# Attention scores from the queries as loaded: two 64x64 products per pair of heads in place of one 128x128 product, and a reordered second half of attention

## The chip, the cores and the metric

The kernel runs on one core of a Trainium2 chip as one program. The metric is the device time of that core in microseconds, the median over several runs, compared between kernels on the same chip. Engines are called as the profile calls them: PE (matrix products, with its weight loads PEld), DVE, ACT, POOL, and SP, which here only issues DMAs.

## What is computed

Three layers in a row, all in float32. First a local attention with block summaries, for 2 batches, 8 heads, 768 positions and head width 64:

```python
k_sum = k.reshape(B, H, nb, 32, D).max(axis=3)
v_sum = v.reshape(B, H, nb, 32, D).mean(axis=3)
scores_l = where(abs(i - j) < 16, scale * q @ k.T, -1e9)
scores_s = scale * q @ k_sum.T + log(32)
a = softmax(concat([scores_l, scores_s]))
x = a @ concat([v, v_sum])
```

Its rows become 1536 tokens of width 512. Then a mixture of 8 experts with one expert per token, `relu(x @ w1[e]) @ w2[e]` times two gates (widths 512, 1024, 512). Then a gated layer on all tokens, `(sigmoid(x @ w_gate) * (x @ w_val)) @ w_out` (widths 512, 1536, 512).

## The kernel before

**The program.** There is no scheduler: every engine executes its instructions in the order in which the Python code issues them, and waits on semaphores where data or buffers are not ready. Attention is the first sixth of the time. It overlaps with the load and the first steps of the experts. After it come seven blocks of up to 256 tokens each through an expert (`item_A` is the first product, `item_B` the second), and then the gated layer.

**Attention** goes over 12 tiles T of 128 queries (6 per batch), for all 8 heads. A tile has two halves of 64 queries, and each half meets its own 128 columns of keys (96 near keys or padding, and 24 block maxima) which stand in `kg` with two heads over each other: head 2p on partitions 0 to 63, head 2p+1 on 64 to 127. The steps of a tile are small functions:

- `load_q` (lines 226 to 228) brings 128 partitions x 512 queries: two heads over each other, 4 pairs, 2 halves, 64 queries. The buffers lie in `xg`, which later holds the tokens of the experts.
- `spread_q` (230 to 239) copies them, scaled by -0.125, into one of three `qz` buffers, as blocks of 128x128 with zeros in the two off-diagonal quarters. For T = 2 and 3 DVE does it, otherwise ACT, two instructions a tile. POOL zeroes the buffers once (line 833).
- `s1` (302 to 335): per half, a bfloat16 product writes the mask for all 4 pairs into a PSUM bank (line 312, full array), then 4 products of 128x128 by 128 columns add the scores, one for each pair (line 316). DVE takes the minimum (`nm`, line 333) and ACT the exponentials (335). Scores are negative here, so minimum and scale -1 stand for the maximum.
- `s3` (337 to 345): PE transposes the exponentials (`a`, line 344) and ACT copies them to `aT`. Two PSUM banks with the tag B serve these transposes and those of `s6`.
- `s4` (347 to 364): 16 products with 64 columns of weights and 65 moving columns (line 354), which write the upper and the lower 64 partitions of the bank pair C in turn; DVE normalises into `x`.
- `s6` and `s7` (366 to 380): transposes of `x` and the 16 router logits (379).

`place_sums` (281 to 294) turns the block means of v: 8 products with 24 columns of weights and 128 moving columns (line 286), to partitions 32 and 96 in turn.

A float32 product on PE stands as two records in the trace (two passes); transposes and the products of the experts, which use a reduced float32 type, stand as one.

**The loop over T** (856 to 974) runs `s1` two tiles ahead of `s4`. From T = 6 on it also carries the routing of the first batch (`route`, one step per `run(g, 1)`), from T = 7 the choice of the first two expert blocks (`pick_two`, a chain of small DVE instructions) and `find_first`, which finds the token rows of block 0: six comparisons of 128x256 on DVE (602), 12 small products on PE (607), and two gathers on POOL. At T = 10 and 11 the weights of block 0 are split into a high and a low part: `split1(p)` (628) is one ACT copy and one DVE subtraction for a quarter of `w1`. `item_T` transposes the tokens of block 0 for `item_A`.

Of the kernel before, what the change touches and what calls it, by code (L numbers as in the profile page):

```python
# [30 lines left out]
NT = B * TB  # L31
KST = 160
KW = TB * KST + 32
C = 128
# [34 lines left out]
def shape_constants():  # L69
    bf = lambda x: float(np.float32(x).astype(ml_dtypes.bfloat16))  # L70
    c = 8.0 * math.log(BLK)
    parts = []
    for _ in range(3):
        parts.append(bf(c))
        c -= parts[-1]
    mask = np.zeros((67, 4, C), np.float32)
    for v, t in ((0, 0), (1, 2), (2, 1), (3, 2 * TB - 1)):
        for c in range(C):
            col = col_start(t) + c
            k = key_of(col)  # L80
            if is_sum(col):
                mask[64:67, v, c] = [-0.125 * x for x in parts]
            elif k is None:
                mask[:64, v, c] = 1.0e9
            else:
                q = t * 64 + np.arange(64)
                mask[:64, v, c] = np.where(np.abs(q - k) < WIN, 0.0, 1.0e9)
    sel = np.zeros((67, 128), np.float32)
    sel[np.arange(128) % 64, np.arange(128)] = 1.0
    sel[64:] = 1.0  # L90
    m = np.zeros((80, 4 * C + 128), ml_dtypes.bfloat16)
    m[:67] = np.concatenate([mask.reshape(67, -1), sel], axis=1)
    kb = np.ones((128, CKB), ml_dtypes.bfloat16)
    kb[:, 0:128] = np.triu(np.ones((128, 128)), 1)
    kb[:, 256:256 + SLOT] = np.arange(SLOT)
    token = np.stack(np.broadcast_arrays(np.arange(128)[:, None], 128 * np.arange(TB)), axis=2)
    kb[:, 256 + SLOT:256 + SLOT + 2 * TB] = token.reshape(128, 2 * TB)
    k = np.zeros((128, 128), np.float32)
    e = np.arange(E)
    k[:, 0:8] = E - e  # L100
    k[:, 16:24] = e
    k[:, 24:88] = np.broadcast_to(np.arange(8)[None, :] * float(SLOT), (E, 8)).reshape(-1)
    k[:, 88:101] = np.arange(13)
    k[:, 101:114] = SLOT * np.arange(13)
    k[:, 114:127] = NTOK + SLOT * np.arange(13)
    return m, k, kb, np.eye(128, dtype=np.float32)


def moe_kernel(tc, A, out):
# [107 lines left out]
    qz = {}  # L217
    st = {}

    qbuf = [at.tile([128, 4, 2, 128], F32, name=f"qz{k}") for k in range(3)]  # L220
# [8 lines left out]

    def spread_q(T):  # L230

        qz[T] = qbuf[T % 3]
        src = q_raw(T).rearrange("p (g h q) -> p g h q", g=4, h=2)
        for j in range(2):
            s = slice(64 * j, 64 * j + 64)
            if 1 < T < 4:
                ts(qz[T][s, :, :, s], src[s], -0.125, ALU.mult)
            else:
                SC.mul(qz[T][s, :, :, s], src[s], -0.125)
# [62 lines left out]
    def s1(T, halves=(0, 1)):  # L302
# [11 lines left out]
        def score(half, pr):  # L314
            c0 = col_start(2 * m + half)
            PE.matmul(sc[half][:, pr], qz[T][:, pr, half], kg[b][:, pr, c0:c0 + C], start=False, stop=pr == 3)
# [9 lines left out]
        for half in halves:  # L326
            if T:
                mask(half)
                for pr in range(4):
                    score(half, pr)  # L330
            scv = sc[half]
            nm = at.tile([128, 4], F32, tag="nm", bufs=4, name=f"nm{T}{half}")
            pace.append(red(nm, scv, ALU.min))
            for pr in range(4):
                SC.activation(out=a[:, half * 4 + pr], in_=scv[:, pr], func=AF.Exp, bias=nm[:, pr:pr + 1], scale=-1.0)
# [260 lines left out]
    def find_first():  # L596
# [6 lines left out]
        yield  # L603
# [220 lines left out]
    with tc.manual_schedule():  # L824
# [7 lines left out]
        for t in qbuf:  # L832
            G.memset(t, 0.0)
# [16 lines left out]
        spread_q(0)  # L850
        spread_q(1)
# [3 lines left out]
        spread_q(2)  # L855
        for T in range(NT):
# [3 lines left out]
            if T < 2:  # L860
# [7 lines left out]
                if T == 1:  # L868
                    spread_q(3)
            else:  # L870
                if T < NT - 1:
                    s3(T)
                if T == 3:
                    spread_q(5)
# [3 lines left out]
                if T == NT - 1:  # L878
                    item_T(0, 0, ("A", 3))
                    item_T(0, 1, ("A", 3))  # L880
                    s4(T)
                    now = ()
                for t in q8:
                    s7(t)
                for t in now[:-1]:
                    s4(t)
                for t in first:
                    s1(t, (0,))
                for t in q6:
                    s6(t)  # L890
                if 2 < T < NT - 3:
                    spread_q(T + 3)
                for t in first:
                    s1(t, (1,))
                if T == 2:
                    spread_q(4)
                if T == 3:
                    ksum(1, 1)
                if T == 8:
                    run(ff, 9)  # L900
                if T > 8:
                    run(g, 1)
            for t in now[-1:]:
                s4(t)
            for t in then:
                s1(t)
# [8 lines left out]
            if T == 1:  # L915
# [3 lines left out]
                load_q(7)  # L919
# [12 lines left out]
            if T == 2:  # L932
                ksum(1, 0)
# [3 lines left out]
            if 2 < T < 7:  # L937
                load_q(T + 5)
            if T == 4:
                place_sums(1)  # L940
# [16 lines left out]
            if T == 7:  # L957
# [4 lines left out]
                run(ff, 1)  # L962
# [5 lines left out]
            if T == 10:  # L968
                split1(1)
                split1(2)  # L970
            if T == 11:
                run(g, 9)
                load_w(reg["e", 0], None, range(4, 8))
                split1(3)
# [10 lines left out]
        item_A(0)  # L985
        s6(11)
        item_A(1)
        run(p1, 1)
        item_gather(0, gidx[:, 16], S)
        item_gather(1, gidx[:, 17], S)  # L990
        item_A(2)
        s7(11)
        item_A(3)
# [263 lines left out]
```

## Time and profile before

| | |
|---|---|
| time of 3 runs | 551.37, 552.43, 552.91 us; median 552.43 |
| the profiled execution | 552.51 us, of which the trace spans 550.7 |
| PE busy | 535.1 us, 97% of the span |
| DVE, ACT, POOL busy | 386.8, 213.0, 124.7 us |
| granted PE clock, mean over the span | 0.994 of full speed |

The profile names a group of equal instructions by line, engine, operation and tiles. A busy PE is modelled: records last longer than the step from one to the next, so the pace of PE is read from the starts of neighbouring groups, not from the length of a record. In a timeline the bracket behind a row is the idle time of that engine before it and what ended it.

### The profile page before, as it was taken

The page shows a single profiled execution, that of the slowest core. Times are in us where ns is not written, and L with a number is a line of the kernel's source. Part 1 is how long each engine was busy: PE and PEld are TensorE (multiplying, and loading weights), DVE is VectorE, ACT ScalarE, POOL GpSimd, SP SyncE. Part 2 cuts the span into 40 slices and gives each one's busy share as a digit, 9 for nine tenths or more (in the row PEclk, how much of TensorE's full clock was granted, in tenths as well). Part 3 has the DMA queues.
Part 4 walks back from the last instruction along what each step waited for, and adds up shares of the span by engine and source line. Part 5 has one row for each costly group of instructions (what it writes and reads, how often), then busy time and mean ns, then how long its engine had stood idle before and what let it go on. Part 6 is the DMA issues. An engine that isn't in the chain of part 4 may idle for free.

```text
span 550.7 us, 8927 instructions
## 1 busy us (share of the span) xinstructions
PE 535.1 (97%) x3236; PEld 456.3 (83%) x3236; DVE 386.8 (70%) x737; ACT 213.0 (39%) x390; POOL 124.7 (23%) x151
## 2 busy tenths in 40 slices
PE   7999999999999999999999999999999999999995
PEld 4789989888989989878888888888888888888884
DVE  5785876898778677853878899999998753323330
ACT  3776683655546455643221221211111442122110
POOL 3656054072101101000010111102101152212211
PEclk9999998999999999999999999999999999999998
DMA  8994286971569403216132323323322000001001
GB/s 323 412 411 144 84 279 218 333 281 39 176 252 297 136 12 118 72 56 211 39 114 78 114 80 111 115 81 112 114 76 77 1 2 38 20 38 39 21 37 39
DMA packets 31984, 71.63 MB, mean 130 GB/s; under 512 B 3056, under 2 KB 11712, under 8 KB 31936
## 3 DMA queue, kind: packets, MB, share of 16 engines
q1 hardware_dynamic: 28816, 60.96, 32.1%
q0 software_dynamic: 3120, 10.06, 5.4%
q8 instruction: 26, 0.43, 0.3%
q14 instruction: 22, 0.18, 0.1%
HBM read 72.53 MB, written 11.33 MB: 152 GB/s over the span
## 4 chain that ended last, share of the span: by engine, by line
PE 34%; issue 15%; POOL 5%; ACT 0%; POOLq 0%; DVE 0%; DVEq 0%; ACTq 0%
PE ps_A L1141 18%; PE ps_B L1141 15%; POOL out_dram L1189 3%; POOL yb L134 2%; PE ps_B L746 1%; POOLq L1253 0%; ACT yb L131 0%; ACT gs L131 0%; DVE gg L137 0%; POOLq L1189 0%; DVEq L137 0%; POOLq L134 0%; ACTq L131 0%
## 5 line engine op out<-in xcount | busy, mean ns | idle before, releaser
L1182 PE MATMUL ps_A<-yb,gs 128*128 128x512 f32 x432 | 98.1, 389 | 0.0
L1141 PE MATMUL ps_A<-yb,wh 128*128 128x512 f32 x312 | 96.9, 392 | 0.1
L1182 PEld LDWEIGHTS ps_A<-yb,gs 128*128 128x128 f32 x432 | 81.1, 188 | 16.8
L1141 PE MATMUL ps_B<-yb,wh 128*128 128x512 f32 x264 | 81.3, 389 | 0.0
L1141 PEld LDWEIGHTS ps_A<-yb,wh 128*128 128x128 f32 x312 | 57.9, 188 | 12.0 <-issue 0.6
L1141 PE MATMUL ps_A<-yb,wl 128*128 128x512 f32 x156 | 60.8, 389 | 0.0
L1141 PEld LDWEIGHTS ps_B<-yb,wh 128*128 128x128 f32 x264 | 49.5, 188 | 10.2
L134 POOL TENSOR_TENSOR wl<-cvw,wh 128x512 fp32r<-128x512 f32 x20 | 26.7, 1334 | 137.8 <-ACT wh L131 137.8
L1150 ACT ACTIVATE sg<-ps_A 128x512 f32<-128x512 f32 x36 | 21.5, 596 | 91.2 <-PE ps_A L1141 91.2
L652 PE MATMUL ps_A<-xTh,w1h 128*128 128x256 f32 x192 | 55.4, 289 | 1.0 <-DVE hl L655 1.0
L652 PE MATMUL ps_A<-xTl,w1h 128*128 128x256 f32 x192 | 54.8, 286 | 0.0
L652 PE MATMUL ps_A<-xTh,w1l 128*128 128x256 f32 x192 | 54.8, 286 | 0.0
L1141 PE MATMUL ps_B<-yb,wl 128*128 128x512 f32 x132 | 51.3, 389 | 0.0
L131 ACT ACTIVATE gs<-gg 128x768 fp32r<-128x768 f32 x24 | 20.3, 847 | 69.5 <-PE ps_A L1182 67.4
L134 DVE TENSOR_TENSOR gs<-gg,gs 128x768 fp32r<-128x768 f32 x24 | 23.0, 958 | 34.2 <-ACT gs L131 34.1
L143 DVE TENSOR_SCALAR cva<-cva 128x512 f32<-128x512 f32 x72 | 43.4, 602 | 1.9
L134 DVE TENSOR_TENSOR w2l<-w2r,w2h 128x1024 fp32r<-128x1024 f32 x28 | 34.2, 1224 | 9.9 <-ACT w2h L131 9.6
L661 PE MATMUL yp<-w2h,hh 128*128 128x512 f32 x96 | 39.0, 406 | 0.0
L652 PEld LDWEIGHTS ps_A<-xTh,w1h 128*128 128x128 f32 x192 | 37.3, 194 | 1.6 <-DVE hl L655 1.4
L661 PE MATMUL yp<-w2h,hl 128*128 128x512 f32 x96 | 37.6, 391 | 0.0
L652 PEld LDWEIGHTS ps_A<-xTl,w1h 128*128 128x128 f32 x192 | 37.4, 195 | 0.2
L661 PE MATMUL yp<-w2l,hh 128*128 128x512 f32 x96 | 37.5, 391 | 0.0
(232 smaller groups left out, 959.3 us busy)
## 6 DMA issues: line engine op xcount, KB each, us to landing
w1r<-in_w_dram SPq DMA_DIRECT2D x28, 512.0 KB
w2r<-in_w_dram SPq DMA_DIRECT2D x28, 512.0 KB
raw<-in_wgv_dram SPq DMA_DIRECT2D x24, 512.0 KB
vt<-in_vv_dram SPq DMA_DIRECT2D x12, 520.0 KB
raw<-in_wo_dram SPq DMA_DIRECT2D x12, 512.0 KB
kg<-in_kg_dram SPq DMA_DIRECT2D x8, 496.0 KB
y_c<-yt SPq DMA_DIRECT2D x13, 256.5 KB
yr<-y_c SPq DMA_DIRECT2D x12, 256.5 KB
```

Source lines behind the costliest of these rows:

```text
L131: SC.activation(out=o, in_=i, func=AF.Copy)
L134: (eng or V).tensor_tensor(out=o, in0=i, in1=h.bitcast(F32), op=ALU.subtract)
L143: V.tensor_scalar(out=o, in0=a, scalar1=s1, scalar2=s2, op0=op0, op1=op1)
L652: PE.matmul(hp, w[:, c, s], x[:, c], start=n == 0, stop=n == 11)
L661: PE.matmul(yp[h], x[:, f, s], w[:, f], start=f == 0 and n == 0, stop=f == 7 and n == 2)
L746: PE.transpose(tp[:, c], r[:, c * 128:c * 128 + 128], ident)
L1141: PE.matmul(pp, w[:, c], x[:, c], start=n == 0, stop=n == 11)
L1150: SC.activation(out=sg, in_=pp, func=AF.Sigmoid)
L1182: PE.matmul(po, g2[:, x, f % 6], yb[f // 4][w][:, f % 4], start=f == 0 and n == 0, stop=f == 11 and n == 2)
L1189: d = G.indirect_dma_start(out=out[:, :], out_offset=bass.IndirectOffsetOnAxis(ap=row_id[:, t:t + 1].bitcast(U32), axis=0), in_=ot, in_off ...
```

## The change

`spread_q`, its three buffers and their zeroing go. Per pair of heads the score is now two products, one for each head, on 64 partitions of the queries as loaded and of the keys: rows 0 to 63 write PSUM partitions 0 to 63, and rows 64 to 127 write partitions 64 to 127 of the same bank. The queries are no longer scaled or negated, so the mask's constants change, the minimum becomes a maximum, DVE multiplies it by -0.125 in an instruction of its own, and the scale of the exponential is 0.125.

Query buffers now stay in use until the scores have been taken, so `load_q(7)` and `load_q(8)` to `load_q(11)` are issued one tile later. The order in the second half of attention changes too: `place_sums(1)` from the end of T = 4 to between the two halves of `s1` at T = 5; the comparisons of `find_first` in two groups of three, each behind a half of `s1` at T = 8, and its products behind `s4(8)`; at T = 10 `s7` between the transposes of tiles 10 and 11; at T = 11 `s4(11)` behind `s7(9)` and `s6(10)`; and the splits 1 to 3 of `w1` into the first items of block 0.

```diff
-                mask[64:67, v, c] = [-0.125 * x for x in parts]
+                mask[64:67, v, c] = parts
-    qbuf = [at.tile([128, 4, 2, 128], F32, name=f"qz{k}") for k in range(3)]
-    def spread_q(T):
...
-            PE.matmul(sc[half][:, pr], qz[T][:, pr, half], kg[b][:, pr, c0:c0 + C], start=False, stop=pr == 3)
+            q = q_raw(T).rearrange("p (g h q) -> p g h q", g=4, h=2)
+            for p0 in (0, 64):
+                r = slice(p0, p0 + 64)
+                PE.matmul(sc[half][r, pr], q[r, pr, half], kg[b][r, pr, c0:c0 + C], start=False, stop=pr == 3)
...
-            pace.append(red(nm, scv, ALU.min))
+            pace.append(red(nm, scv, ALU.max))
+            ts(nm, nm, -0.125, ALU.mult)
...
         for t in range(TB):
             ts(P[:, t], count, first, ALU.add, pf[:, t:t + 1], ALU.is_equal)
-        yield
+            if t % 3 == 2:
+                yield
...
+                if T == NT - 1:
+                    item_T(0, 0, ("A", 3))
+                    item_T(0, 1, ("A", 3))
+                for t in q8:
+                    s7(t)
                 if T == NT - 2:
                     s3(T + 1)
                     split1(0)
-                if T == NT - 1:
-                    item_T(0, 0, ("A", 3))
-                    item_T(0, 1, ("A", 3))
-                    s4(T)
-                    now = ()
-                for t in q8:
-                    s7(t)
                 for t in now[:-1]:
                     s4(t)
                 for t in first:
                     s1(t, (0,))
+                if T == 8:
+                    run(ff, 1)
                 for t in q6:
                     s6(t)
+                if T == 5:
+                    place_sums(1)
                 for t in first:
                     s1(t, (1,))
                 if T == 8:
-                    run(ff, 9)
+                    run(ff, 1)
                 if T > 8:
                     run(g, 1)
             for t in now[-1:]:
                 s4(t)
+            if T == 8:
+                run(ff, 9)
...
-            if 2 < T < 7:
-                load_q(T + 5)
+            if 3 < T < 8:
+                load_q(T + 4)
             if T == 4:
-                place_sums(1)
...
-            if T == 10:
-                split1(1)
-                split1(2)
             if T == 11:
                 run(g, 9)
                 load_w(reg["e", 0], None, range(4, 8))
-                split1(3)
...
         item_A(0)
+        split1(1)
         s6(11)
         item_A(1)
         run(p1, 1)
+        split1(2)
...
         s7(11)
+        split1(3)
         item_A(3)
```

PE at the end of attention, T = 10 and 11, in the order before (`a` exponentials, `xp` the output of `s4`, `late` the tokens, `xT` their transposes, `xg` the tokens of block 0):

```order
L354 MATMUL xp_1202<-vt_111,aT_1148 64x65 x16
L344 MATMUL ps_B<-ident,a_1059 128x128 x8
L344 MATMUL ps_B<-ident,a_1167 128x128 x8
L379 MATMUL ps_A<-wgo,xT_1185 128x16 x4
L370 MATMUL ps_B<-ident,late 128x128 x4
L354 MATMUL xp_1271<-vt_111,aT_1227 64x65 x16
L641 MATMUL ps_A<-ident,xg_87 128x128 x8
L354 MATMUL xp_1313<-vt_111,aT_1240 64x65 x16
L379 MATMUL ps_A<-wgo,xT_1266 128x16 x4
L370 MATMUL ps_B<-ident,late 128x128 x4
```

And the same place in the changed kernel, whose line numbers are smaller by about ten:

```order
L305 MATMUL ps_A<-kg_107,xg_88 64x128 x8
L344 MATMUL xp_1292<-vt_111,aT_1228 64x65 x16
L334 MATMUL ps_B<-ident,a_1124 128x128 x8
L369 MATMUL ps_A<-wgo,xT_1270 128x16 x4
L334 MATMUL ps_B<-ident,a_1247 128x128 x8
L360 MATMUL ps_B<-ident,late 128x128 x4
L344 MATMUL xp_1361<-vt_111,aT_1317 64x65 x16
L632 MATMUL ps_A<-ident,xg_87 128x128 x8
L369 MATMUL ps_A<-wgo,xT_1356 128x16 x4
L360 MATMUL ps_B<-ident,late 128x128 x4
L344 MATMUL xp_1415<-vt_111,aT_1336 64x65 x16
L369 MATMUL ps_A<-wgo,xT_1410 128x16 x4
```

Router logits now stand between the two groups of transposes, and the last `s4` stands one group before the end, with logits on either side of it. The scores (first row) are 8 products of 64x128 where 4 of 128x128 stood.

ACT from the last exponentials to the first products of block 0 before (`w1h` is the high part of a quarter of `w1`, `hh` the output of an `item_A`):

```order
L335 ACTIVATE a_1167<-ps_A,nm_1193 128x128 x4
L345 COPY aT_1227<-ps_B 128x512 x2
L131 ACTIVATE w1h<-w1r 128x4x256
L372 COPY xT_1266<-ps_B 128x512
L131 ACTIVATE w1h<-w1r 128x4x256 x2
L131 ACTIVATE xTh<-ps_A 128x4x128 x2
L372 COPY xT_1345<-ps_B 128x512
L131 ACTIVATE w1h<-w1r 128x4x256
L654 ACTIVATE hh<-ps_A 128x256
```

And in the changed kernel:

```order
L131 ACTIVATE w1h<-w1r 128x4x256
L362 COPY xT_1356<-ps_B 128x512
L131 ACTIVATE xTh<-ps_A 128x4x128 x2
L362 COPY xT_1410<-ps_B 128x512
L645 ACTIVATE hh<-ps_A 128x256
L131 ACTIVATE w1h<-w1r 128x4x256
L362 COPY xT_1487<-ps_B 128x512
L645 ACTIVATE hh<-ps_A 128x256
L131 ACTIVATE w1h<-w1r 128x4x256
L645 ACTIVATE hh<-ps_A 128x256
L131 ACTIVATE w1h<-w1r 128x4x256
```

The second, third and fourth quarter now each stand behind an item's output. DVE's subtractions move in the same way.

DVE at T = 7 and 8 before (`gidx` is the end of `pick_two`, `place` the comparisons and then the row numbers read from them):

```order
L466 SCALAR_TENSOR_TENSOR gidx<-o_gp_1022,o_gr_1021 128x2
L143 TENSOR_SCALAR place<-ckb,o_f_1004,r_pf_1000 128x256 x6
L380 COPY lg<-ps_A 128x16
L146 TENSOR_REDUCE nm_1066<-ps_A 128x4
L146 TENSOR_REDUCE nm_1087<-ps_A 128x4
```

And in the changed kernel:

```order
L456 SCALAR_TENSOR_TENSOR gidx<-o_gp_1094,o_gr_1093 128x2
L370 COPY lg<-ps_A 128x16
L146 TENSOR_REDUCE nm_1135<-ps_A 128x4
L141 TENSOR_SCALAR nm_1135<-nm_1135 128x4
L143 TENSOR_SCALAR place<-ckb,o_f_1076,r_pf_1072 128x256 x3
L146 TENSOR_REDUCE nm_1163<-ps_A 128x4
L141 TENSOR_SCALAR nm_1163<-nm_1163 128x4
L143 TENSOR_SCALAR place<-ckb,o_f_1076,r_pf_1072 128x256 x3
```

The reductions of tile 10 come before the comparisons that stood ahead of them, and each is followed by the new multiplication.

## Rows read from the trace of the kernel before

**Rows 1.** Busy time by stretch: us, PE, PEld, DVE, ACT, POOL, granted clock, DMA, GB/s

```profile
18.00:45.00 27.00, 25.82 (x333) 23.44 (x335) 21.03 (x54) 20.93 (x58) 15.72 (x31) 1.00 0.97 380
45.00:63.00 18.00, 18.00 (x222) 16.80 (x218) 11.07 (x36) 12.51 (x35) 6.02 (x5) 1.00 0.41 131
...
87.10:90.60 3.50, 3.50 (x19) 3.50 (x19) 2.75 (x13) 0.38 (x1) 0.93 (x2) 0.51 0.48 160
...
140.00:550.00 410.00, 403.88 (x1996) 341.05 (x1995) 279.04 (x426) 126.87 (x194) 67.03 (x66) 1.00 0.28 90
```

**Rows 2.** Timeline of PE in a steady tile: start us, us, group

```profile
53.64 1.05 PE L316 MATMUL ps_A<-kg,qz 128*128 128x128 f32 x8
54.53 0.60 PE L370 MATMUL ps_B<-ident,w2r 128*128 128x128 f32 x4
...
55.19 1.05 PE L316 MATMUL ps_A<-kg,qz 128*128 128x128 f32 x8
56.17 1.15 PE L354 MATMUL xp<-vt,aT 128*64 128x65 f32 x32
57.26 1.07 PE L379 MATMUL ps_A<-wgo,xT 128*128 128x16 f32 x8
```

**Rows 3.** Timeline of PE, the block means of the second batch

```profile
44.36 1.06 PE L286 MATMUL sp<-ident,vs 128*24 128x128 f32 x16 [0.33 <-DVE lg L380]
45.35 0.87 PE L344 MATMUL ps_B<-ident,a 128*128 128x128 f32 x6
```

**Rows 4.** Groups up to 87 us, shapes apart: xcount, busy us, mean ns, idle before

```profile
L239 ACT ACTIVATE qz<-xg 64x512 f32<-64x512 f32 x20 | 12.6, 629 | 7.4 <-DMA xg<-in_q_dram 7.2
...
L131 ACT ACTIVATE w1h<-w1r 128x1024 fp32r<-128x1024 f32 x4 | 4.2, 1069 | 0.0
L134 DVE TENSOR_TENSOR w1l<-w1r,w1h 128x1024 fp32r<-128x1024 f32 x3 | 3.6, 1217 | 0.0
...
L141 DVE TENSOR_SCALAR rs<-xp 128x8 f32<-128x8 f32 x12 | 2.0, 164 | 2.4 <-PE xp L354 2.4
```

**Rows 5.** Timeline of PE, three waits in the first half

```profile
18.04 0.84 PE L286 MATMUL sp<-ident,vs 128*24 128x128 f32 x12 [0.92 <-POOL vs L274]
...
23.07 0.66 PE L344 MATMUL ps_B<-ident,a 128*128 128x128 f32 x4 [0.38 <-ACT aT L345]
...
39.92 0.49 PE L316 MATMUL ps_A<-kg,qz 128*128 128x128 f32 x2 [0.44 <-DVE kg L255]
```

**Rows 6.** Timeline of PE, T = 8 and 9

```profile
67.60 1.36 PE L607 MATMUL ps_M<-ckb,place 128*128 128x2 bf16 x12
68.89 1.15 PE L354 MATMUL xp<-vt,aT 128*64 128x65 f32 x32
69.97 0.66 PE L344 MATMUL ps_B<-ident,a 128*128 128x128 f32 x4
70.96 0.66 PE L344 MATMUL ps_B<-ident,a 128*128 128x128 f32 x4 [0.33 <-ACT xT L372]
...
73.75 0.66 PE L370 MATMUL ps_B<-ident,late 128*128 128x128 f32 x4 [0.21 <-ACT aT L345]
```

**Rows 7.** Timeline of DVE, T = 7 and 8

```profile
66.95 1.62 DVE L143 TENSOR_SCALAR place<-ckb,o_f,r_pf 128x256 bf16<-128x256 bf16 x6
...
68.57 1.28 DVE L146 TENSOR_REDUCE nm<-ps_A 128x4 f32<-128x512 f32 x2
```

**Rows 8.** Timeline of PE's weight loads, waits at T = 10 and 11

```profile
78.02 0.91 PEld L344 LDWEIGHTS ps_B<-ident,a 128*128 128x128 f32 x8 [0.63 <-ACT aT L345]
...
82.78 1.04 PEld L354 LDWEIGHTS xp<-vt,aT 128*64 128x64 f32 x32 [0.47 <-PE ps_A L641]
86.17 0.97 PEld L379 LDWEIGHTS ps_A<-wgo,xT 128*128 128x128 f32 x8 [0.97 <-ACT xT L372]
```

**Rows 9.** Timeline of PE, two neighbouring passes of an expert's first product

```profile
91.06 0.28 PE L652 MATMUL ps_A<-xTl,w1h 128*128 128x256 f32 x1
91.18 0.28 PE L652 MATMUL ps_A<-xTh,w1l 128*128 128x256 f32 x1
```

More of the change, by code (lines that the diff above doesn't have):

```diff
@@ L81, in shape_constants @@
             if is_sum(col):
-                mask[64:67, v, c] = [-0.125 * x for x in parts]
+                mask[64:67, v, c] = parts
             elif k is None:
-                mask[:64, v, c] = 1.0e9
+                mask[:64, v, c] = -8.0e9
             else:
                 q = t * 64 + np.arange(64)
-                mask[:64, v, c] = np.where(np.abs(q - k) < WIN, 0.0, 1.0e9)
+                mask[:64, v, c] = np.where(np.abs(q - k) < WIN, 0.0, -8.0e9)
     sel = np.zeros((67, 128), np.float32)
@@ L216, in moe_kernel @@
     vt = {(b, half): p.tile([128, 3, 2, VW], F32, name=f"vt{b}{half}") for b, p in ((0, ft), (1, at)) for half in range(2)}
-    qz = {}
     st = {}
-    qbuf = [at.tile([128, 4, 2, 128], F32, name=f"qz{k}") for k in range(3)]
     def q_raw(T):
@@ L228, in load_q @@
         SP.dma_start(out=q_raw(T), in_=A["q"][b, m])
-    def spread_q(T):
[L232 to L239, printed above, removed]
     def load_k(b, pairs):
@@ L332, in s1 @@
             nm = at.tile([128, 4], F32, tag="nm", bufs=4, name=f"nm{T}{half}")
-            pace.append(red(nm, scv, ALU.min))
+            pace.append(red(nm, scv, ALU.max))
+            ts(nm, nm, -0.125, ALU.mult)
             for pr in range(4):
-                SC.activation(out=a[:, half * 4 + pr], in_=scv[:, pr], func=AF.Exp, bias=nm[:, pr:pr + 1], scale=-1.0)
+                SC.activation(out=a[:, half * 4 + pr], in_=scv[:, pr], func=AF.Exp, bias=nm[:, pr:pr + 1], scale=0.125)
     def s3(T, halves=(0, 1)):
@@ L831, in moe_kernel @@
         load_q(2)
-        for t in qbuf:
-            G.memset(t, 0.0)
         V.memset(warm, 0.0)
@@ L849, in moe_kernel @@
         ahead = {0: ((1,), ()), 1: ((2,), ()), 2: ((3,), ()), 3: ((4,), (5,))}
-        spread_q(0)
-        spread_q(1)
         s1(0)
@@ L854, in moe_kernel @@
             vsum_part(0, c)
-        spread_q(2)
         for T in range(NT):
@@ L867, in moe_kernel @@
                         vsum_part(0, 2 + half)
-                if T == 1:
-                    spread_q(3)
             else:
@@ L872, in moe_kernel @@
                     s3(T)
-                if T == 3:
-                    spread_q(5)
+                if T == NT - 1:
[3 more added lines that the diff above has]
+                    s7(t)
                 if T == NT - 2:
@@ L888, in moe_kernel @@
                     s1(t, (0,))
+                if T == 8:
+                    run(ff, 1)
                 for t in q6:
                     s6(t)
-                if 2 < T < NT - 3:
-                    spread_q(T + 3)
+                if T == 5:
+                    place_sums(1)
                 for t in first:
                     s1(t, (1,))
-                if T == 2:
-                    spread_q(4)
                 if T == 3:
@@ L918, in moe_kernel @@
                     load_vr(1, c)
-                load_q(7)
                 load_v(1, 0)
@@ L932, in moe_kernel @@
             if T == 2:
+                load_q(7)
                 ksum(1, 0)
@@ L961, in moe_kernel @@
                 item_regs(0)
-                run(ff, 1)
                 load_w(reg["e", 0], None, range(4))
```

## The prediction

> **What bounds the kernel now.** I read the busy time by stretch first, since a share over the whole span mixes stages. From 18 to 45 us PE works 25.8 of 27 us, from 45 to 63 all of it, from 140 to 550 us 403.9 of 410 [rows 1]. DVE and ACT have room in these stretches. So attention is bound by PE, and what PE gains or loses there reaches the end, because after it PE alone fills the time. The same view shows one stretch of another kind: from 87.1 to 90.6 us the granted clock is 0.51, the lower of the two levels (1.2 of 2.4 GHz), with 19 products in 3.5 us, right after the thinnest piece of PE work in attention.
>
> Next I read PE's timeline in a steady tile, by the starts of groups. Eight passes of the scores go from 53.64 to 54.53: 0.89 us, 0.11 a pass. The same eight, followed by the narrow products of `s4`, take from 55.19 to 56.17: 0.98 us [rows 2]. The 0.09 between them is what PE pays to go from the full array to a part of it. `s4` itself, half an array wide, puts 32 passes with 65 columns into 1.09 us (56.17 to 57.26), 0.034 a pass.
>
> Last come PE's waits, as brackets in the timelines. In the first half: 0.92 for POOL's block sums, 0.38 for ACT's `aT`, 0.44 for DVE's key maxima [rows 5], 0.33 for the second batch's block sums [rows 3]. In the second half: the row-finding products, which hold PE from 67.60 to 68.89 for 12 tiny products, then 0.33 and 0.21 for ACT [rows 6], and at T = 10 and 11 weight loads that wait 0.63, 0.47 and 0.97 [rows 8].
>
> **The change, part by part.**
>
> *The products.* Per half, 4 products of 8 passes become 8 products of 16 passes, each on a quarter of the array. No trace row has a 64x64 tile, so I bound it. The nearest row is the block means: 128 moving columns as in the scores, two narrow tiles in turn, 16 passes from 44.36 to 45.35, with the return to the full array in it: 0.99 us [rows 3]. That is 0.062 a pass, so two tiles run beside each other, but a pair takes as long as one full-array pass. By this row the scores take 0.87 us as before, and the change into the tile (0.09 [rows 2]) and back (0.99 less 8 x 0.11 = 0.11, I take 0.10) are added. The lower bound is the pace of `s4`, 0.034; the upper bound is no overlap, 0.11 a pass.
> Rows 3 also has two tiles that write one PSUM bank side by side, on different partitions, though both use all rows. The Trainium skill (TensorEngine Tiling, Restrictions and Gotchas) says that different row tiles cannot access the same PSUM bank at the same time. The two score tiles are different row tiles and write one bank: by that rule the sum would rise by about 20 us (second rival), by the row it does not. No row of this trace shows two row tiles.
>
> *Where it counts.* Up to 18.04 us PE's lateness is swallowed by the 0.92 us wait for POOL [rows 5], whose sums depend on DMA alone: five tile changes of tiles 1 and 2 (0.5 us) and the new multiplication fit in it. Behind it stand 19 halves, each with a change into the tile (19 x 0.09 = 1.7), and 11 that are followed by full-array work (11 x 0.10 = 1.1; the other 8 are followed by `s4`, which pays a change today). **+2.8**, between 0 and 30 x 0.12 = 3.6.
>
> *The multiplication by -0.125* is 24 small DVE instructions; the nearest is 0.164 [rows 4], some 0.2 with its handover. PE feels it only where it waits for what lies behind: at 23.07 (the exponentials stand ahead of `aT` on ACT) and at 39.92 [rows 5], before which DVE has done six of them since 23 us. There PE's lateness of about 1 us and DVE's of 6 x 0.2 = 1.2 overlap, so 0.2 remains. **+0.4.**
>
> *The spread* leaves ACT with 20 instructions of 0.629 less, 12.6 us [rows 4]. Worth almost nothing by itself: PE waits for the spread 0.1 us behind the start. I count **-0.1**. POOL's zeroing ran in the time in which POOL waits for DMA: nothing. The query loads that go one tile later on SP still have about two tiles before their scores, and the one that now stands ahead of the expert weights delays these by one short issue, long before their first split: nothing. If that cover went, the cost would be one issue, some tenths.
>
> *Block means of batch 2* move behind ready data: the bracket of 0.33 plus the handover goes, **-0.4**. POOL's copies of the means come some 4 us later, and their first reader is more than a tile away.
>
> *The row finding at T = 8.* DVE's chain, not PE, sets this place. Today the comparisons start at 66.95, end at 68.5, and both reductions follow [rows 7]. In the new order one logit copy (0.1), two reductions (1.3), two multiplications (0.4) and the comparisons (1.6) end near 70.4. PE does `s4(8)` meanwhile, ends that at 68.8 and then still waits: the transposes that start at 69.97 [rows 6] start near 70.7, +0.7. Because reduction and exponentials are earlier and the spread is gone from ACT's queue, the stops at 70.96 (0.5 in starts) and 73.75 (0.4) go. **-0.2.**
>
> *T = 10 and 11.* The wait of 0.63 at 78.02 [rows 8] is filled by router logits, but then `s6`'s transposes need a bank B that DVE has yet to copy from tile 11: 0. The waits of 0.47 and 0.97 go, since logits and transposes stand ahead of the last `s4`, and `s4` ahead of the last logits: **-1.3**.
>
> *The splits in block 0.* Its third item needs quarter 1 of `w1`. ACT's copy (1.07) and DVE's subtraction (1.22) [rows 4] now start behind item 0's output: with handovers (0.5, my estimate) 2.8 us behind its last product. PE has 4 transposes (0.44), item 1 (12 passes of 0.12 [rows 9]) and two passes to do in that time, 2.1 us. **+0.7** of waiting. Quarters 2 and 3 have an item more of cover.
>
> *The clock.* With the two waits gone, and `s4` in the middle of that piece, I expect no fall at 87: half of 3.5 us at half speed [rows 1], less what was short, **-1.6**.
>
> Sum: 2.8 + 0.4 - 0.1 - 0.4 - 0.2 - 1.3 + 0.7 - 1.6 = +0.3 on the profiled execution's 552.51, which stands 0.08 above the median: **552.8 us**, no change. (0.3% of the time, 1.7 us, is about what a measurement of this kernel can tell from none.)
>
> **Rivals.**
>
> *The clock falls all the same*, at 87 or elsewhere: the thin piece keeps its 16 logit passes, and the scores now use half the array. Then 1.6 us come back: **554.4**, slower. For it: before the fall PE mostly had transposes, logits and half-array products, and these stay [rows 6, 8]. Against it: the waits among them go. 16%.
>
> *The two tiles do not overlap.* 16 passes at 0.11 instead of 0.062: 0.88 us more for each of 24 halves, less the 0.9 hidden at 18.04: +20, **573**. It decides as soon as a score half takes over 1.3 us. For it stands the rule above; against it rows 3, and `s4` in rows 2. 7%.
>
> *Changing the tile is free*, because the small weights are loaded early or the first tile starts while the last full pass drains: the 2.8 us go, **550.0**. Against it the 0.09 in rows 2, which is a change to another shape, though. 18%.
>
> *Tiles run at the pace of `s4`*: 16 x 0.034 = 0.55 and 0.19 for the changes, 0.74 instead of 0.89, over 19 halves -2.9 instead of +2.8: **547.1**. Against it: 65 columns move there, 128 here. 10%.
>
> *The split holds up block 0 for longer*, with quarters 2 and 3 late as well (DVE has two chains of `pick_two` between them): **555**. 7%.
>
> **How the numbers follow.** The forecast holds with 42%. Faster are free changes and quick tiles, 28%; slower are the clock, no overlap and the splits, 30%. The range goes from 546.5 (quick tiles, and some tenths more of waits gone) to 557 (clock and splits together) and leaves out no overlap and the ends, some 15%. The likeliest case alone spans 551 to 554.
>
> **What would show it.** Right: a score half followed by transposes takes 0.95 to 1.05 us from start to start where it took 0.89, and the mask ahead of it stands 0.09 longer; the scores have 12 x 2 x 16 = 384 records; the clock is 1.00 from 81 to 91 us; block 0's third item waits for DVE's `w1l`; PE still waits for `place`. The prediction is wrong if a score half takes 0.75 or less or 1.7 or more, if the clock view shows a second low stretch, or if the start of block 0 moves by over 2 us against 87.1 [rows 1].

## The result and the profile after

The changed kernel takes **556.73 us** (median of 5 runs, 556.0 to 558.5) where the kernel before takes 552.43 (5 runs): a ratio of 1.0078, with a 95% interval of 1.0058 to 1.0098. It is slower by some 4.3 us. The time lies inside the predicted range, but the likeliest case, no change, did not come. The profiled execution took 558.26 us (span 556.4), 1.5 above the median.

Where it went is read by setting the starts of the same groups of PE side by side:

| group of PE | before | after | later by |
|---|---|---|---|
| transposes behind the first block means | 18.81 | 19.73 | 0.9 |
| `s4(1)` | 26.31 | 28.31 | 2.0 |
| first `s4` of T = 4 | 37.33 | 40.05 | 2.7 |
| second `s4` of T = 4 | 41.88 | 46.64 | 4.8 |
| `s4(5)` | 49.62 | 55.51 | 5.9 |
| `s4(7)` | 61.92 | 68.53 | 6.6 |
| transposes of tile 10 | 76.53 | 83.62 | 7.1 |
| first product of block 0 | 87.09 | 93.50 | 6.4 |
| logits of tile 11, in block 0 | 93.46 | 99.22 | 5.8 |
| end of the span | 550.7 | 556.4 | 5.7 |

From block 0's fourth item on the distance stays within 0.1 us up to the end. So attention decides, as the prediction had it [rows 1]; the size came out otherwise. The first 0.9 is not shown to belong to the change: PE comes to the first mask of tile 1 at 13.30 us here and at 11.89 in the profile of before, but at 13.32, 13.67 and 13.72 in the three experiments below that keep the old scores.

The pace of the products, in the timeline of PE in a steady tile of the changed kernel (start us, us, group):

```profile
59.31 0.38 PE L298 MATMUL ps_A<-cmb 67*128 67x512 bf16 x1
59.62 1.09 PE L305 MATMUL ps_A<-kg,xg 64*64 64x128 f32 x16
60.65 0.66 PE L360 MATMUL ps_B<-ident,w2r 128*128 128x128 f32 x4
61.14 0.38 PE L298 MATMUL ps_A<-cmb 67*128 67x512 bf16 x1
61.45 1.09 PE L305 MATMUL ps_A<-kg,xg 64*64 64x128 f32 x16
62.47 1.15 PE L344 MATMUL xp<-vt,aT 128*64 128x65 f32 x32
```

From mask to mask's scores it is 0.31, which was 0.22; from the scores to the transposes 1.02, which was 0.89, and to `s4` also 1.02, which was 0.98 [rows 2]. So a half costs 0.22 more where full-array work follows, and 0.13 more where `s4` does.

The two stops at the key maxima, which answer to the third of [rows 5], in the same view:

```profile
41.46 0.65 PE L305 MATMUL ps_A<-kg,xg 64*64 64x128 f32 x8
42.55 0.44 PE L305 MATMUL ps_A<-kg,xg 64*64 64x128 f32 x4 [0.44 <-DVE kg L241]
43.90 0.44 PE L305 MATMUL ps_A<-kg,xg 64*64 64x128 f32 x4 [0.91 <-DVE kg L241]
```

One stop of 0.44 became two, 1.35 in sum. Right behind them the clock falls. The busy time by stretch (us, PE, PEld, DVE, ACT, POOL, granted clock, DMA, GB/s):

```profile
45.00:48.50 3.50, 3.50 (x49) 3.05 (x48) 2.11 (x5) 1.83 (x7) 0.00 (x0) 0.57 0.20 51
...
81.00:91.00 10.00, 8.85 (x126) 7.81 (x126) 6.45 (x15) 6.38 (x15) 5.78 (x7) 1.00 0.67 238
```

The low stretch of [rows 1] is gone from 87 us, and one like it stands from 45.5 to 48.9. Half of 3.4 us at the lower level is 1.7.

Why DVE is late with the maxima is seen in its timeline, two pieces of it:

```profile
37.90 0.68 DVE L146 TENSOR_REDUCE nm<-ps_A 128x4 f32<-128x512 f32 x1
38.62 0.87 DVE L141 TENSOR_SCALAR nm<-nm 128x4 f32<-128x4 f32 x1
39.40 0.68 DVE L146 TENSOR_REDUCE nm<-ps_A 128x4 f32<-128x512 f32 x1
40.12 0.17 DVE L141 TENSOR_SCALAR nm<-nm 128x4 f32<-128x4 f32 x1
...
41.26 0.97 DVE L137 TENSOR_TENSOR ks<-kt 128x6 f32<-128x6 f32 x1
42.26 0.23 DVE L241 COPY kg<-ks 128x144 f32<-128x144 f32 x1
```

and in POOL's at the same times:

```profile
38.46 1.01 POOL L258 TENSOR_TENSOR w1r<-w1r 128x384 f32<-128x384 f32 x1
...
41.20 1.00 POOL L258 TENSOR_TENSOR w1r<-w1r 128x384 f32<-128x384 f32 x1
```

The new multiplication of 128x4 elements takes 0.17 in one of these rows and 0.87 in the other. The long one starts just after a sum of POOL and ends (39.49) when that ends (39.47); the small maximum at 41.26 ends (42.23) with the next (42.20). The Trainium skill (SBUF — State Buffer, Who interferes with whom) says that DVE and POOL share a pair of ports which the one that starts first holds for its whole instruction, that a `tensor_scalar` can take the pair, and that an operation with both inputs in SBUF contends with POOL's reads. The timing in the trace agrees; which port an instruction uses it does not show.

The other waits in this trace, which answer to [rows 5, 6, 8]:

```profile
24.66 0.66 PE L334 MATMUL ps_B<-ident,a 128*128 128x128 f32 x4 [0.77 <-ACT aT L335]
...
55.51 1.15 PE L344 MATMUL xp<-vt,aT 128*64 128x65 f32 x32 [0.23 <-ACT vt L276]
...
76.40 0.84 PE L598 MATMUL ps_M<-ckb,place 128*128 128x2 bf16 x9 [0.38 <-DVE place L143]
...
86.09 1.14 PE L334 MATMUL ps_B<-ident,a 128*128 128x128 f32 x8 [0.57 <-ACT aT L335]
87.53 0.66 PE L360 MATMUL ps_B<-ident,late 128*128 128x128 f32 x4 [0.30 <-DVE aT L335]
...
97.92 0.39 PE L643 MATMUL ps_A<-xTh,w1l 128*128 128x256 f32 x1 [0.62 <-DVE w1l L134]
```

0.38 became 0.77 at the second `aT`, a wait for `vt` is new, the place of the row finding is down to one short wait, and block 0 waits for its split.

**The clock and the single execution.** Each run comes with its mean granted clock. Of the 25 runs of the kernel before beside the first four experiments, 15 had a mean of 0.996 or more (median 551.9) and 10 less (553.6). Of the 11 runs of the changed kernel (5 here, 6 of a later repeat) 7 had 0.996 or more, 4 less. So a fall like that of [rows 1] happens in a part of the executions only, and about as often in both kernels; where it lies, the mean does not tell. It does not make the difference: the runs at 0.996 or more have medians of 551.9 and 556.4, the others 553.6 and 557.9.

### The profile page after: what moved, and what is told of

Its sections match the earlier page's. It is cut to its first block, busy times and chain, and to the rows that moved or that the text cites. A ratio compares the mean times of both kernels' runs of the same rounds, so it can differ in the third digit from the quotient of the medians.

```text
span 556.4 us, 9324 instructions
## 1 busy us (share of the span) xinstructions
PE 540.8 (97%) x3428; PEld 452.4 (81%) x3428; DVE 390.9 (70%) x757; ACT 201.5 (36%) x370; POOL 122.5 (22%) x148
## 4 chain that ended last, share of the span: by engine, by line
PE 34%; issue 14%; POOL 5%; ACT 0%; POOLq 0%; DVE 0%; DVEq 0%; ACTq 0%
PE ps_A L1120 18%; PE ps_B L1120 15%; POOL out_dram L1168 3%; POOL yb L134 2%; PE ps_B L737 1%; POOLq L1232 0%; ACT yb L131 0%; ACT gs L131 0%; DVE gg L137 0%; POOLq L1168 0%; DVEq L137 0%; POOLq L134 0%; ACTq L131 0%
## 5 line engine op out<-in xcount | busy, mean ns | idle before, releaser
L1120 PE MATMUL ps_A<-yb,wh 128*128 128x512 f32 x312 | 96.8, 392 | 0.1
L325 ACT ACTIVATE a<-ps_A,nm 128x128 f32<-128x128 f32 x96 | 27.1, 374 | 37.9 <-DVE nm L141 29.6
```

What stands on the lines that cost most here:

```text
L1120: PE.matmul(pp, w[:, c], x[:, c], start=n == 0, stop=n == 11)
```

## The experiments

All ran beside the kernel before; ratios are to that, with 95% intervals. Two theories stood at the start: the products with their multiplication cost it all and the order is a gain, or the order itself costs.

**The order alone.** The kernel before, with the changed kernel's places of `place_sums(1)`, `find_first`, T = 10 and 11 and the splits:

```diff
+                if T == 5:
+                    place_sums(1)
...
+            if T == 8:
+                run(ff, 9)
...
         item_A(0)
+        split1(1)
```

> The kernel before with the new order alone: spread queries, one product of 128x128 per pair and its query loads as before; the places of place_sums(1), find_first, T = 10 and 11 and of the three splits as in the changed kernel. Theory (the new order is a gain and the products with their multiplication cost it all): 549.5 to 551.5, 1 to 3 us under before, since the low clock at 87 us is gone, as are some 2 us of waits, against 0.8 us of waiting for a split in block 0. Rival (the order itself costs, by the split and by the copies that now stand after the last exponentials): 553.5 to 556.

Measured: 552.48 us, ratio 0.9995 (0.9976 to 1.0014). The order alone is worth nothing, not 2 us, and costs nothing either. 7 of the 12 runs had a mean clock under 0.996, the profiled one had not; at like clock the order is 0.7 to 0.8 under the kernel before (551.1 and 551.9, 552.9 and 553.6), too little to be sure of. Its timeline shows three waits on PE that use up most of the gains:

```profile
50.21 1.16 PE L354 MATMUL xp<-vt,aT 128*64 128x65 f32 x32 [0.70 <-ACT vt L290]
...
79.22 1.14 PE L344 MATMUL ps_B<-ident,a 128*128 128x128 f32 x8 [1.11 <-ACT aT L345]
...
91.05 0.39 PE L653 MATMUL ps_A<-xTh,w1l 128*128 128x256 f32 x1 [0.62 <-DVE w1l L134]
```

The block means now stand right ahead of `s4`, and both write the one bank pair with the tag C: `s4` waits until ACT has moved the means to `vt`.

**The scores alone.** The changed kernel with the order of before, the inverse of the diff above.

> The changed kernel with the order of before (place_sums(1), find_first, T = 10 and 11, splits): the 64x64 products, the multiplication and the later query loads alone. Theory: 557 to 560, since tile changes cost 0.25 us a half that full-array work follows and 0.13 one that s4 follows (some 4 us), the multiplication on DVE 0.5 us at the exponentials of tile 2 and about 1 us at the key maxima, and the clock falls twice, near 45 and near 87 us. Rival (the order made the changed kernel slow): 553 to 555.

Measured: 559.77 us, ratio 1.0130 (1.0098 to 1.0161), the time as expected. But the profile has one fall of the clock where two were expected: from 93.4 to 96.8 us, at the start of block 0 as in [rows 1]. Near 45 there is none (granted clock 1.00 from 44 to 52), though the two stops stand right ahead of it:

```profile
42.61 0.44 PE L305 MATMUL ps_A<-kg,xg 64*64 64x128 f32 x4 [0.33 <-DVE kg L241]
43.95 0.43 PE L305 MATMUL ps_A<-kg,xg 64*64 64x128 f32 x4 [0.90 <-DVE kg L241]
```

All 6 runs had a mean clock under 0.996; the profiled one, at 0.995, took 558.57, the changed kernel's at 0.995 558.26. So with the new scores the new order shows in how often the clock falls, and in little else.

**The multiplication on ACT.**

```diff
-            ts(nm, nm, -0.125, ALU.mult)
+            SC.mul(nm, nm, -0.125)
```

> The changed kernel with the multiplication by -0.125 on ACT, ahead of the exponentials, instead of on DVE; nothing else. Theory (on DVE it is held until POOL's running instruction ends, 0.4 to 0.9 us at five places, and this reaches PE at the second aT wait and at the key maxima): 553.5 to 555.5; the waits for kg near 42 us go from 1.35 to under 0.6 in all, the multiplication on ACT takes about 0.2 each time, and the low clock near 45 us may go with the wait. Rival (the multiplication is off the path, only the tile changes count): 556.2 to 557.2, no difference.

Measured: 554.81 us, ratio 1.0047 (1.0027 to 1.0067): about 1.7 less than the changed kernel by the ratios, whose intervals just overlap; 11 of 12 runs had a clock of 0.996 or more. The group of the 24 multiplications (xcount, busy us, mean ns, idle before) in the changed kernel, and then in this one:

```profile
L141 DVE TENSOR_SCALAR nm<-nm 128x4 f32<-128x4 f32 x24 | 6.3, 264 | 0.8
```

```profile
L323 ACT ACTIVATE nm<-nm 128x4 f32<-128x4 f32 x24 | 5.1, 213 | 30.1 <-DVE nm L146 30.0
42.17 0.43 PE L305 MATMUL ps_A<-kg,xg 64*64 64x128 f32 x4 [0.93 <-DVE kg L241]
```

On ACT each takes 0.205 to 0.247, never longer. One stop at `kg` remains, 0.93 where under 0.6 was expected, though the maxima ahead of it are not held here (0.16 and 0.15); the wait for `aT` is 0.58.

**The key maxima earlier.** Two of the four of batch 2 move one place up on DVE:

```diff
                 if T == 3:
-                    ksum(1, 1)
+                    ksum(1, 2)
...
                 load_q(7)
                 ksum(1, 0)
+                ksum(1, 1)
             if T == 3:
-                ksum(1, 2)
                 ksum(1, 3)
```

> The changed kernel with two of the four key maxima of batch 2 one place earlier on DVE (the second at the end of T = 2, the third inside T = 3; the fourth stays): PE finds kg ready at 42 us. Theory (the stop at kg costs 1.35 us and also brings the low clock behind it): 553 to 554.8, with a clock of 1.00 from 44 to 49 us. Rival (the clock falls all the same, for the half-array work around it): 555 to 555.6. Rival (what waits at kg is given back at the next wait): 556.2 to 557.2.

Measured: 556.48 us, ratio 1.0060 (1.0038 to 1.0082), not told apart from the changed kernel. In its profile the stop at `kg` is 0.21 and the clock stays at 1.00 inside attention, so PE is 2.7 us earlier at block 0; two thirds of that are lost in block 0 and at the start of block 1, first here:

```profile
107.40 0.17 PE L405 MATMUL ps_M<-cum,ckb 128*128 128x16 bf16 x1 [0.83 <-DVE cum L146]
```

Why ACT and DVE were late there is open. 7 of the 8 runs had a clock of 0.996 or more, so the clock does not hide a gain. By time the run does not show that the stop costs anything; it is repeated below in a better place.

**The changed kernel once more**, as it is.

> The changed kernel itself once more, beside the runs that follow, to see what differs from execution to execution. Theory (what the first profile shows belongs to the kernel): 555.5 to 557; POOL's sums of batch 2 again run until 43 to 44 us, multiplications on DVE that meet them again take 0.4 to 0.9 us, and the two stops at kg add up to 1 to 1.5 us. What belongs to the execution: the later start (up to 1 us by the first transposes) and whether the clock falls inside attention (about 1.7 us in the executions that have it).

Measured: 556.97 us, ratio 1.0075 (1.0047 to 1.0102). Its profile has the same long instructions (a multiplication of 0.88 and a maximum of 0.97 at 39 and 41 us), the same two stops (0.84 and 1.18 us from the start of the last pass before a stop to the next one, in the first profile 0.71 and 1.18) and the low clock from 44.7 to 48.1. What differs: a standstill of PE of 0.50 us in the middle of `s4(9)`, which no wait explains, is not there, nor is the wait of 0.57 for `aT`, and PE reaches block 0 1.0 us earlier.

**Both halves in one piece**, with the multiplication on ACT:

```diff
-        for half in halves:
-            if T:
+        if T:
+            for half in halves:
                 mask(half)
+            for half in halves:
                 for pr in range(4):
                     score(half, pr)
+        for half in halves:
...
-                    s1(t, (0,))
+                    s1(t)
...
-                for t in first:
-                    s1(t, (1,))
```

> The changed kernel with the multiplication on ACT (as in the run with the scale on ACT, 554.81) and, from tile 3 on, both halves of a tile's scores in one piece: two masks, then 32 passes on the small tiles, then the transposes of s6 that stood between the halves. This takes away one change into the small tile and one out of it for 8 tiles, and one pair more for tile 5. Theory (each change in costs 0.09 to 0.10, each way out to full-array work 0.15): 9 x 0.24 = 2.1 less, 552.2 to 553.4; two halves together take 2.4 from the first mask to the next group where they took 2.66 in two pieces. Rival (the changes are real but the maxima of the first half now come later, and PE waits for aT instead): 554 to 555.5.

Measured: 556.95 us, ratio 1.0096 (1.0068 to 1.0124), slower than with the multiplication on ACT alone and above both expected ranges. The piece itself got shorter, as expected, but the gain came back as waits:

```profile
24.10 0.60 PE L298 MATMUL ps_A<-cmb 67*128 67x512 bf16 x2
24.63 1.96 PE L305 MATMUL ps_A<-kg,xg 64*64 64x128 f32 x32
26.53 0.66 PE L362 MATMUL ps_B<-ident,w2r 128*128 128x128 f32 x4
...
51.56 1.15 PE L346 MATMUL xp<-vt,aT 128*64 128x65 f32 x32 [1.41 <-ACT vt L276]
...
66.92 0.66 PE L336 MATMUL ps_B<-ident,a 128*128 128x128 f32 x4 [0.69 <-ACT xT L364]
```

24.10 to 26.53 is 2.43, against 1.33 for each of two separate halves. ACT now has eight exponentials in a row, and PE waits for the copies that stand behind them. This profiled run took 554.09 with no fall of the clock inside attention; 4 of the 6 runs had a lower clock, three of them 0.990 or 0.991, and these make the median; so how much the joining costs by itself stays open.

**The old scores with a part of the order.** As the run with the order alone, but `place_sums(1)` back at the end of T = 4 and `split1(1)` at T = 10.

> The kernel before, spread queries and all, with a part of the new order: find_first's comparisons and products as in the changed kernel at T = 8, the order at T = 10 and 11, and splits 2 and 3 in block 0; but place_sums(1) stays at the end of T = 4 and split 1 at T = 10. Theory (in the run with the order alone, the order at T = 8 gave 0.9, that at T = 10 and 11 gave 0.8, place_sums cost 0.2 and the split 0.85; the low clock near 87 us goes as well): 549.8 to 551.2, under both kernels. Rival (split 1 at T = 10 delays the copies of aT and xT on ACT by 1.1 us and takes the gain back): 551.8 to 553.

Measured: **549.62 us**, ratio 0.9958 (0.9943 to 0.9972), faster than both kernels; 10 of 11 runs at a clock of 0.996 or more. Against before, PE gains 0.9 at T = 8 and 9, and 1.4 at T = 10 and 11. There, where the run with the order alone waited 1.11:

```profile
77.06 0.96 PE L379 MATMUL ps_A<-wgo,xT 128*128 128x16 f32 x8
77.87 1.07 PE L344 MATMUL ps_B<-ident,a 128*128 128x128 f32 x8
79.29 0.66 PE L370 MATMUL ps_B<-ident,late 128*128 128x128 f32 x4 [0.35 <-DVE aT L345]
```

**One tile after the other.** The changed kernel with the four products on rows 0 to 63 first, then the four on rows 64 to 127:

```diff
-                for pr in range(4):
-                    score(half, pr)
+                for p0 in (0, 64):
+                    for pr in range(4):
+                        score(half, pr, (p0,))
```

> The changed kernel with the 8 products of a half in another order from tile 1 on: first the four on rows 0 to 63, then the four on rows 64 to 127, so that neighbours use the same tile. Theory (two tiles run beside each other only where neighbours in the queue use different ones): 16 passes at 0.109 instead of 8 pairs at 0.109, 0.87 us more for 22 halves, 573 to 577. Rival (the overlap does not hang on the order, or there is none): 555.5 to 558.

Measured: 563.26 us in 2 runs, ratio 1.0203 (1.0165 to 1.0240). Slower by some 6.5 than the changed kernel, so the order of neighbours matters, but by well under half of what was expected. The group:

```profile
52.42 1.58 PE L305 MATMUL ps_A<-kg,xg 64*64 64x128 f32 x16
53.93 1.09 PE L361 MATMUL ps_B<-ident,w2r 128*128 128x128 f32 x8
```

A half takes 1.51 where it took 1.02: 0.49 more, not 0.87. The starts of its 16 records in the same trace, in us. The records do not name their rows; those with a star are put down to the second tile, since they go on in steps of 0.109 among themselves, as the others do:

```
52.421  52.582  52.691  52.800  52.909  52.915*  53.019  53.075*
53.128  53.184*  53.236  53.293*  53.402*  53.511*  53.621*  53.730*
```

Read so, the second tile does not wait for the first to be done: its first pass starts beside the fifth of the first tile's eight, four of each run side by side, and four are left over at 0.109.

**POOL's sums in shorter pieces.** The changed kernel, batch 2's additions cut at 96 elements:

```diff
-                G.tensor_tensor(out=t[:, :, 0:n], in0=t[:, :, 0:n], in1=t[:, :, n:2 * n], op=ALU.add)
+                k = 96 // n if b and n > 4 else NB
+                for j in range(0, NB, k):
+                    G.tensor_tensor(out=t[:, j:j + k, 0:n], in0=t[:, j:j + k, 0:n], in1=t[:, j:j + k, n:2 * n], op=ALU.add)
```

> The changed kernel with POOL's block sums of batch 2 cut into shorter instructions: those of 1.00 us into four, those of 0.61 into two, each then some 0.39 long, the same additions. DVE is as in the changed kernel. Theory (a small DVE instruction from SBUF to SBUF waits until POOL's running instruction ends): between 32 and 47 us none of these on DVE takes over 0.6 us, where 0.87 and 0.97 were seen; the two stops at kg fall from 1.35 to under 0.9 in sum; 555.3 to 556.6. Rival (POOL's load on the memory slows DVE, in proportion to its busy time): the same stretches stay, POOL being busy for longer, and the time is 556.5 to 558.

Measured: 554.06 us, ratio 1.0037 (1.0021 to 1.0053), an interval apart from the changed kernel's 1.0058 to 1.0098, though nothing was changed on PE, DVE or ACT, and POOL does more instructions. 6 of 7 runs had a clock of 0.996 or more. The timelines of DVE, POOL and PE:

```profile
38.41 0.17 DVE L141 TENSOR_SCALAR nm<-nm 128x4 f32<-128x4 f32 x1
...
39.22 0.29 DVE L141 TENSOR_SCALAR nm<-nm 128x4 f32<-128x4 f32 x1
...
40.49 0.15 DVE L137 TENSOR_TENSOR ks<-kt 128x6 f32<-128x6 f32 x1
```

```profile
39.09 2.96 POOL L260 TENSOR_TENSOR w1r<-w1r 128x96 f32<-128x96 f32 x8
```

```profile
42.40 0.43 PE L307 MATMUL ps_A<-kg,xg 64*64 64x128 f32 x4 [0.27 <-DVE kg L241]
```

0.87 and 0.97 are gone with POOL as busy as ever, and PE's stop is 0.27. So it is the length of POOL's single instruction that holds DVE, not POOL's load. The time is under the 555.3 to 556.6 expected: the gain of 2.3 is more than the 1.08 that the stops lost. This profile also has no fall of the clock near 45 us, no standstill in `s4(9)` and no wait of 0.57 for `aT`; how much of the rest each of these gives is open.

**The new scores in the same part of the order**, with the multiplication on ACT:

> The 64x64 products with their multiplication on ACT, in exactly the order of the run with the old scores and a part of the new order (549.62): the difference of the two is what the products cost by themselves. Theory (changes of tile at 19 halves behind the first waits: 11 x 0.24 and 8 x 0.13 = 3.7, less the tenths that the freed spread gives): 552.6 to 553.8. Rival (half of that is hidden behind waits that stand anyway): 551 to 552.

Measured: 552.94 us, ratio 1.0020 (1.0008 to 1.0032), all 12 runs at 0.996 or more. Against the old scores in the same order (549.62) the products, with a multiplication that POOL does not hold, cost **3.3 us**. In the two profiles PE is 3.45 us apart behind block 0. Waits are in it: at `kg` 0.79 against 0.27, at the second `aT` 0.57 against 0.38, while the old scores alone wait 0.38 for `place`.

**The same two with the key maxima earlier**, the diff as above:

> The same with two of the four key maxima of batch 2 one place earlier on DVE. Theory (the stop at kg of 0.9 goes, and nothing else waits in its place): 0.5 to 0.9 less than the run without, 552 to 553. Rival (the maxima delay the reductions in front of the exponentials of tile 4, and PE waits there): no less, 552.8 or more.

> The spread queries with the part of the new order (549.62) and the key maxima one place earlier. Theory: the stop at kg near 40 us (0.15 to 0.45) goes, 549.0 to 549.6. Rival (it comes back as a wait for aT, or DVE's spread of tiles 2 and 3 stands in the way): 549.6 to 550.5.

Measured: 551.68 us, ratio 0.9992 (0.9976 to 1.0008), for the new scores, and **549.05 us**, ratio 0.9952 (0.9933 to 0.9970), for the old, the lowest median, though not told apart from the 549.62. The stop at `kg` of the run with the new scores, and the same place with the maxima earlier:

```profile
42.23 0.44 PE L305 MATMUL ps_A<-kg,xg 64*64 64x128 f32 x4 [0.79 <-DVE kg L241]
```

```profile
40.43 1.09 PE L305 MATMUL ps_A<-kg,xg 64*64 64x128 f32 x16
41.46 0.66 PE L360 MATMUL ps_B<-ident,w2r 128*128 128x128 f32 x4
```

With the multiplication off DVE the stop vanishes and the time follows, by 1.3. The new scores can be had at the time of before (551.7), but in both of these orders the old ones are faster, by 3.3 and 2.6 us.

## Why the prediction was right and wrong

**By its own signs.** The signs of being right came: a half in 1.02, its mask 0.31 after the mask's start, 384 records, a clock of 1.00 from 81 to 91 us, the wait of the third item for `w1l` and that for `place`. One of the signs of being wrong came too: block 0 starts at 93.50 against 87.09, 6.4 us later and not within 2. That the time lies inside the range is in part luck. The range reached up to 557 for a clock that falls and late splits; what filled it was the multiplication, a clock term that was not there to be gained, and block means that gave nothing.

**The products: right in kind, a little too small.** The step said that two tiles run beside each other at the pace of the block means and that only the changes of tile cost. That holds: 16 passes take the time of 8, on one bank. The term of +2.8 measured 11 x 0.22 + 8 x 0.13 = 3.5 by starts, and 3.3 and 2.6 as times of two pairs of runs. The way in was right (0.09); the way out was taken as 0.10, but the first pair also takes 0.16 instead of 0.11. The wait of 0.92 that was to swallow the changes of tiles 1 and 2 belongs to one execution: in the three other profiles with the old scores PE comes to these block means at 18.1 us or later, and no pass of theirs starts over 0.41 after the one before it. The rivals are decided: the tiles do overlap, the change is not free, the pace of `s4` is not reached, and block 0 waits for one quarter only. The rule of the Trainium skill (TensorEngine Tiling (Array Packing), Restrictions and Gotchas) that different row tiles cannot access one bank at the same time would have made it 573; here they write one bank, on different partitions, and a pair starts every 0.109, so the measurement decides against it. Another sentence of the Trainium skill (TensorEngine Tiling (Array Packing), Tiling Modes, Key Properties) is that a change of the tiling mode drains the engine; the 0.22 is in line with it, but what the engine does in that time no trace here shows.

**The multiplication: the step that failed.** It said 0.2 each, and +0.4. Its price came from a row of like size (128x8) and the same name, `rs<-xp` [rows 4], whose input is in PSUM; one of these took 0.16 at 39.78 in the middle of a sum of POOL (39.64 to 40.30). The new instruction goes from SBUF to SBUF. 7 of 24 took over 0.3 us, and each of these ended within 0.03 us of the end of an instruction of POOL that had started before it. Two of them fell where PE waits: one at the second `aT` (0.38 to 0.77) and one, with a held key maximum behind it, at `kg` (0.44 to 1.35). Without it (on ACT) the kernel is 1.7 us faster, with POOL's instructions cut short 2.3. The kernel before has rows that would have told: two copies of key maxima on DVE, the first with POOL idle and the second beside its sums:

```profile
29.89 0.23 DVE L255 COPY kg<-ks 128x144 f32<-128x144 f32 x1
...
34.15 0.64 DVE L255 COPY kg<-ks 128x144 f32<-128x144 f32 x1
...
33.03 2.48 POOL L272 TENSOR_TENSOR w1r<-w1r 128x384 f32<-128x384 f32 x4 [5.61 <-DMA w1r<-in_vr_dram]
```

**The clock: -1.6 was wrong twice.** The fall at 87 us went, as said, in every profiled execution with the new order; but with the order alone 7 of 12 runs had a mean under 0.996, so the order does not keep the clock up. In the changed kernel a fall came at 45 us instead, behind the new stops, so the first rival's "elsewhere" is what its profile shows. And the term could not have been worth 1.6 in a median, for before has the low mean in 10 of 25 runs only: one profiled execution was taken for all. That a stop brings the fall is not shown: the run with the scores alone had the same two stops and no fall behind them. With one stop or none at `kg` a low mean was rare in these runs (1 of 12 with the scale on ACT, none of 12 with the new scores in a part of the order, with and without the earlier maxima), but the order alone stops there for 0.15 only and has a low mean in 7 of 12. What brings it is open.

**Block means, -0.4:** wrong. The step looked for the readers of the copies, and overlooked that `s4` writes the same bank: a wait for `vt` (0.70 in the order alone, 0.23 here) took the place of the one removed.

**T = 8, -0.2:** better than said, 0.9 with the old scores. **T = 10 and 11, -1.3:** right where it ran undisturbed (1.4 in the run with a part of the order); in the changed kernel only 0.7, because of the wait of 0.57 for `aT` which the repeat does not have. **The splits, +0.7:** right, a bracket of 0.62, and 0.90 from start to start where a step takes 0.12; putting the first of them back is a part of what made the best kernels. **The spread, -0.1:** no run takes it away by itself.

The sum of the parts as measured: the order 0, the products 2.6 to 3.3, the multiplication 1.7 to 2.3, together 4.3 to 5.6, where the whole measured 4.3 with an interval of about 1.1 to each side. The parts come from different runs and share waits, so the sum is a check and no proof.

## What to carry to other kernels

Price a small DVE instruction by where its operands lie and by what POOL runs at that moment, not by its size: SBUF to SBUF beside a long POOL instruction costs up to that instruction's length, and moving it to ACT or cutting POOL's work into shorter pieces takes the cost away. Quartering the array saves nothing when the pair takes as long as one full pass did (0.109 us both), and every change of the tile's shape is paid on both sides. Before a low clock, or a wait that is to cover something, is put into a sum, look at how many runs have it.

## What the runs showed that was not expected

- A multiplication of 128x4 on DVE took 0.17 us alone and 0.87 beside a sum of POOL of 1.01, and ended with it.
- Two row tiles wrote one PSUM bank side by side, a pair every 0.109 us. Issued one tile after the other, the second, as its starts are read above, began beside the fifth pass of the first and ran beside its last four, so that 16 passes took 1.51 us with the way out instead of 1.02.
- PE stood still for 0.50 us in the middle of `s4(9)` in the changed kernel (and for 0.51 and 0.56 in two of the experiments), with no wait that the trace names; DMA moved 352 GB/s from 82.5 to 84 us. In the repeat of the same kernel it did not. What holds it is open.
